# Attention, a mixture of experts and a maxout block on one core: where weight sums, conversions, Sinkhorn and pieces of expert 0 are placed

## The chip, the cores and the metric

One core of one Trainium2 chip. The metric is the device time of one execution in microseconds; the kernel of before was timed three times. Changes of less than about 0.2% are not told from no change.

## The reference

```python
attn = softmax(scale * q @ k.T + bias, local window and global keys) @ v     # 2 x 8 heads x 768 x 64
x = attn.transpose(0, 2, 1, 3).reshape(1536, 512)
logits = x @ w_gate; P = exp(logits - logits.max())                          # 1536 x 8
for _ in range(8):                                                           # Sinkhorn
    P /= P.sum(1, keepdims=True) + 1e-9
    P /= P.sum(0, keepdims=True) + 1e-9
    P *= N / E
out = sum(P[:, e:e+1] * (relu(x @ w1[e]) @ w2[e]) for e in range(8))         # 512 -> 1024 -> 512
h = max(out @ m1, out @ m2, out @ m3); y = h @ w_out                         # 512 -> 768 -> 512
```

The last block's weights come as 64-bit floats in memory and are turned into 32-bit floats on the chip.

## The kernel before

Every matmul factor is split into a high part (a copy, rounded to fp32r, on ScalarE) and a low part (the rest, by a subtraction: `lower`), and a product of two factors is three matmuls.

**The front** (`near_attention`, 49 steps s) runs the attention. From step 9 on, each of its steps takes one piece of **expert 0** from the list `todo`: `e0_pieces(tb, ...)` gives for one block `tb` of 256 tokens four pieces of the first matrix (24 matmuls of 256 columns) and then pieces of the second (`mm2`; in the front 4 pieces of 12 matmuls of 512 columns). Blocks 0 to 3 run wholly in the front. Of block 4 only the first matrix does, so the last four steps (45 to 48) have no piece. Block 5, and the second matrix of block 4, come after the front; their hidden values lie in columns of `xh`/`xl` that belonged to tokens done with.

**The main part** is an order written out by hand, in slots s. Experts 1 to 7 (two passes over halves of the tokens, p = 0 and 1, 28 groups each) and the last block (p = 2 and 3, 9 groups each) form groups G = 0 to 73. A group multiplies a 2 x 2 block matrix in the Strassen-Winograd way: seven products (`product`, line 1130) of 6 matmuls of 384 columns, at slots 7G + 0, 2, 4, 8, 10, 12, 13 (`REL`). Products 1, 2 and 4 take raw blocks of the weights (`sb`), products 3, 5, 6 and 7 take sums of them (`sa`, needed first at slot 7G + 4). With two groups in flight nearly every slot holds one product. After a slot's product come its hooks (`at(slot, f, pri)`, lower pri first) and then at most one **filler**, in order, from the slot it is due: first the 16 pieces (6 matmuls of 512 columns) of expert 0 that were left over, from slot 24 on the second matrices of experts 1 to 7 (`y_piece`, 12 per 14 slots, the last at slot 411), then 6 transposes (`x2_tile`), and late ones of the output (`o_piece`). From slot 412 to 462 hardly a filler is due.

For group G: `s_add` (slot 7G - 7) makes the four sums on POOL from the raw buffer into a tile of their own, `s_raw` (slot 7G - 5) splits the raw blocks, `s_sum` (slot 7G - 1) splits the sums; `lower` is on VectorE, for the raw blocks of p >= 2 on POOL. All loads go through one list of jobs, sorted by slot, on the SP queue: `feed` issues the next job while fewer than 4 of the 4 buffers `raw` are taken and the job's slot of readiness has come; `done` gives a buffer back and feeds.

`convert` (24 times, lines 1078 to 1104: eight VectorE instructions and a store, spread over 6 slots) turns a half of a 64-bit weight block into 32 bits, one every 7 slots from slot 15. `chain_at(p, ...)` makes four differences t1 to t4 of blocks of the tokens for pass p on POOL (line 366) in four raw buffers within 7 slots and stores them; `put` splits them for use at the pass's start (`base` = slots 0, 196, 392, 455).

**Sinkhorn**: `sink_max` (a maximum on VectorE, `partition_all_reduce` on POOL, line 902) stands after the third piece of block 5, `sink_start` at slot 4, and turn n has a small matmul `col` (line 917, into a bank of the pair b2) one slot before `turn` (lines 920 to 893 on VectorE), at slots 6 to 24, two or three apart. The first `y_piece` ends at slot 26 with an instruction that reads the result `pm`. `scale` (POOL, line 1307) multiplies expert 0's output by its column of `pm`, for the first six tiles all at slot 25.

## Time and profile before

| | |
|---|---|
| median of 3 runs | 1410.22 us (1408.98 to 1411.53) |
| the profiled execution | 1409.96 us, span 1408.0 us |
| TensorE (PE) busy | 1329.5 us, 94% of the span |
| VectorE (DVE), ScalarE (ACT), POOL busy | 921.2, 703.9, 673.3 us |
| mean granted TensorE clock | 0.971 of full speed |
| moved by DMA | 147.66 MB, 105 GB/s in the mean |

The span runs from the first to the last instruction; about 2 us of the execution lie outside it. PE is the engine that is nearly always busy, so what counts is where it is not, and which engine it waits for there. A clock of 1.00 in a row is 2.4 GHz, 0.50 is 1.2 GHz.

### The profile page before, as it was taken

To read this page: it belongs to the slowest core of one execution; us is meant where nothing else is said; L and a number is where in the kernel's file an instruction comes from. 1 tells how busy PE (TensorE), PEld (TensorE's weight loads), DVE (VectorE), ACT (ScalarE), POOL (GpSimd) and SP (SyncE) were. 2 spreads that over 40 slices of the span, in tenths; PEclk is the share of its full clock that TensorE was granted. 3 is DMA by queue.
4 is the path that set the end of the run, shared out by engine and by line. 5 is a ranking of instruction groups with operands and counts; after the bars stand their busy time and mean duration, and the time that the engine had idled before them with its cause. 6 is when DMAs were issued, how large, how long until landed. Compare 5 with 4: busy or idle time off the path is not lost.

```text
span 1408.0 us, 19757 instructions
## 1 busy us (share of the span) xinstructions
PE 1329.5 (94%) x6984; PEld 1199.3 (85%) x6984; DVE 921.2 (65%) x1513; ACT 703.9 (50%) x1415; POOL 673.3 (48%) x746
## 2 busy tenths in 40 slices
PE   5899997979999969999999999999999999988988
PEld 3789996768898868888898988889898888887977
DVE  7977875578899969898855444545454546465361
ACT  6877774444445424444465445444444455434341
POOL 5554663226445554445444433346334444595461
PEclk8899997999999989999999999999999999999999
DMA  4633532313333353334333222225211224344111
GB/s 154 180 110 96 165 124 65 120 57 113 105 123 120 111 171 113 114 120 128 121 108 105 60 90 76 76 67 159 88 61 60 64 89 138 98 146 147 60 46 45
DMA packets 59627, 147.66 MB, mean 105 GB/s; under 512 B 6016, under 2 KB 23680, under 8 KB 59520
## 3 DMA queue, kind: packets, MB, share of 16 engines
q1 hardware_dynamic: 59520, 146.32, 33.2%
q8 instruction: 57, 0.93, 0.3%
q14 instruction: 50, 0.41, 0.1%
HBM read 124.27 MB, written 22.02 MB: 104 GB/s over the span
## 4 chain that ended last, share of the span: by engine, by line
PE 82%; DVE 7%; POOL 5%; ACT 2%; DMA 2%; issue 2%; SPq 0%; POOLq 0%; DVEq 0%; ACTq 0%
PE yp L238 40%; PE b L1130 31%; PE hp L221 5%; PE o L592 2%; POOL sum L989 2%; PE t L566 2%; PE s L506 1%; POOL sbl L961 1%; DMA raw<-w 1%; POOL xl L154 1%; DVE w2l L961 1%; DVE sal L961 1%; PE lp L297 0%; DVE sbl L961 0%; DVE etl L574 0%
## 5 line engine op out<-in xcount | busy, mean ns | idle before, releaser
L154 POOL TENSOR_TENSOR xl<-u,xh 128x384 fp32r<-128x384 f32 x112 | 124.0, 1108 | 395.7 <-ACT xh L153 394.6
L238 PE MATMUL yp<-w2h,xl 128*128 128x512 f32 x744 | 296.1, 398 | 0.0
L238 PE MATMUL yp<-w2l,xh 128*128 128x512 f32 x744 | 294.8, 396 | 0.0
L238 PE MATMUL yp<-w2h,xh 128*128 128x512 f32 x744 | 290.9, 391 | 0.0
L1138 ACT COPY u<-b 128x384 f32<-128x384 f32 x148 | 70.9, 479 | 204.5 <-PE b L1130 201.8
L238 PEld LDWEIGHTS yp<-w2h,xl 128*128 128x128 f32 x744 | 140.1, 188 | 29.9
L989 POOL TENSOR_TENSOR sum<-raw 128x256 f32<-128x256 f32 x148 | 121.9, 845 | 76.9 <-DVE sal L961 48.1
L238 PEld LDWEIGHTS yp<-w2h,xh 128*128 128x128 f32 x744 | 140.7, 189 | 18.4
L238 PEld LDWEIGHTS yp<-w2l,xh 128*128 128x128 f32 x744 | 140.2, 188 | 18.4
L1228 DVE SCALAR_TENSOR_TENSOR y<-yp,pm,y 128x512 f32<-128x512 f32 x168 | 124.6, 742 | 28.9 <-PE yp L238 28.8
L961 DVE TENSOR_TENSOR w2l<-raw,w2h 128x1024 fp32r<-128x1024 f32 x62 | 90.6, 1461 | 64.4 <-ACT w2h L1013 64.4
L226 DVE SCALAR_TENSOR_TENSOR xl<-b,xh 128x384 fp32r<-128x384 f32 x56 | 31.1, 555 | 121.6 <-ACT xh L225 120.9
L154 POOL TENSOR_TENSOR xl<-s,xh 128x384 fp32r<-128x384 f32 x56 | 64.4, 1150 | 78.7 <-ACT xh L153 69.0
L961 DVE TENSOR_TENSOR sal<-sum,sah 128x1024 fp32r<-128x1024 f32 x74 | 95.3, 1288 | 8.9 <-ACT sah L995 8.9
L1158 ACT ACTIVATE s<-s 128x384 f32<-128x384 f32 x56 | 29.5, 526 | 140.7 <-DVE s L1178 140.7
L1138 ACT COPY s<-b 128x384 f32<-128x384 f32 x74 | 35.5, 479 | 125.4 <-PE b L1130 125.2
L1178 DVE TENSOR_TENSOR u<-b,u 128x384 f32<-128x384 f32 x136 | 74.8, 550 | 30.6 <-PE b L1130 30.6
L1178 DVE TENSOR_TENSOR s<-b,s 128x384 f32<-128x384 f32 x68 | 37.4, 551 | 76.4 <-PE b L1130 76.2
L995 ACT CAST sah<-sum 128x1024 fp32r<-128x1024 f32 x74 | 77.3, 1045 | 4.9 <-POOL sum L989 4.9
L989 POOL TENSOR_TENSOR sum<-raw,sum 128x256 f32<-128x256 f32 x74 | 73.9, 999 | 5.8
L1013 ACT CAST w2h<-raw 128x1024 fp32r<-128x1024 f32 x62 | 64.9, 1047 | 9.5 <-DMA raw<-w 9.4
L461 POOL TENSOR_TENSOR k<-kqv,k 128x384 fp32r<-128x384 f32 (+1 forms) x46 | 47.1, 1025 | 46.7 <-ACT k L460 46.7
(276 smaller groups left out, 3689.4 us busy)
## 6 DMA issues: line engine op xcount, KB each, us to landing
raw<-w SPq DMA_DIRECT2D x154, 512.0 KB, 3.6
kqv<-a SPq DMA_DIRECT2D x32, 416.0 KB, 3.3
raw<-xt SPq DMA_DIRECT2D x16, 384.0 KB, 3.3
w<-cb SPq DMA_DIRECT2D x24, 256.0 KB, 2.4
raw<-x2d SPq DMA_DIRECT2D x14, 384.0 KB, 3.3
xt<-raw SPq DMA_DIRECT2D x12, 384.0 KB, 2.6
kqv<-a SPq DMA_DIRECT2D x14, 320.0 KB, 3.1
w0r<-w SPq DMA_DIRECT2D x8, 512.0 KB, 3.9
```

The lines of the kernel that those rows point to most:

```text
L154: lo_eng.tensor_tensor(out=lo, in0=src, in1=hi.bitcast(F32), op=ALU.subtract)
L221: nc.tensor.matmul(ps, a[:, q], b, start=k == 0, stop=k == 11)
L238: nc.tensor.matmul(ps, a, b, start=kf == first and i == 0, stop=kf == last and i == 2)
L461: nc.gpsimd.tensor_tensor(out=kb[:, 0:nk], in0=rk, in1=ka[:, 0:nk].bitcast(F32), op=ALU.subtract)
L961: (eng or nc.vector).tensor_tensor(out=l, in0=src, in1=h.bitcast(F32), op=ALU.subtract)
L989: nc.gpsimd.tensor_tensor(out=o, in0=a, in1=b, op=op)
L995: nc.scalar.copy(h, r)
L1013: nc.scalar.copy(h, r)
L1130: nc.tensor.matmul(s[BANK[m]], a[:, c], b[:, kk], start=k == 0 and m in FIRST, stop=k == 5 and m in LAST, skip_group_check=True,)
L1138: nc.scalar.copy(t, st[G]["b1"])
L1178: nc.vector.tensor_tensor(out=o, in0=s[b], in1=s[nm], op=ALU.add)
L1228: nc.vector.scalar_tensor_tensor(out=y[n], in0=ps, scalar=pm[:, n, e : e + 1], in1=y[n], op0=ALU.mult, op1=ALU.add)
```

## The change

- **Sums in place.** `sum_up` makes the four sums in the raw buffer itself, in an order that needs no other tile, so the blocks of sums stand in another order (`PROD`). `s_raw` now comes first (slot 7G - 7), `s_add` at 7G - 5, `s_sum` at 7G - 2, and the raw buffer is held until then. The tile of sums goes and a fifth raw buffer takes its place.
- **Sums of the last block ahead.** For its nine weight blocks the sums are made once, during the passes (`sums_m`, slots 50, 78, ..., 274: a load, four POOL instructions, a store to `w32s`), and each of the 18 last groups loads them as a second job instead of adding. The low part of the sums goes to POOL for every third of these groups.
- **Conversions** come every 14 slots instead of 7 (slots 15 to 337).
- **Chains** of passes 1 and 2 take one difference every 28 slots, that of pass 3 one every 4; each difference loads its two blocks anew (eight loads instead of four).
- **Sinkhorn**: `sink_max` stands first after the front, `sink_start` ahead of slot 0, the `col`s at slots 1, 4, 7, 10, 13, 17, 20, 24 in bank b3, each `turn` first among the hooks of the next slot. `scale` of the first six tiles is spread over slots 25 to 35.
- **Expert 0**: block 4's second matrix runs in the front (4 pieces, steps 45 to 48); block 5's 8 pieces are due at slots 0, 2, ..., 14.

```diff
@@ -244,9 +244,10 @@
     def e0_pieces(tb, php, pyp):
         box = {}
         ws = [w0[4 + j][0] for j in range(4)]
-        if tb >= 4:
-            f = slice((tb - 4) * 2048, (tb - 3) * 2048)
-            box["h"], box["l"] = [t[:, f].rearrange("p (f n) -> p f n", f=8) for t in (xh, xl)]
+        if tb == 5:
+            box["h"], box["l"] = [
+                t[:, 0:2048].rearrange("p (f n) -> p f n", f=8) for t in (xh, xl)
+            ]
 
         def mm1(i):
             def go():
@@ -633,7 +634,7 @@
                         if tb < 5:
                             l1, l2 = logits(tb, ps_h)
                             p1, (p2, _) = e0_pieces(tb, lambda: ps_h, lambda: ps_y)
-                            pcs = p1 + p2 if tb < 4 else p1
+                            pcs = p1 + p2
                             todo += [l1, pcs[0], l2] + pcs[1:]
                             light = (l1, l2)
                 split_qk(s + 2)
@@ -821,13 +822,13 @@
             for tb in range(6):
                 for go in logits(tb, ps_h):
                     go()()
-            for tb in range(5):
-                p1, (p2, _) = e0_pieces(tb, lambda: ps_h, lambda: ps_y)
-                for go in p1 + p2 if tb < 4 else p1:
-                    go()()
             for f in chain0():
                 if f:
                     f()
+            for tb in range(5):
+                p1, (p2, _) = e0_pieces(tb, lambda: ps_h, lambda: ps_y)
+                for go in p1 + p2:
+                    go()()
 
 
     with tc.If(far == 0) as cmp:
@@ -842,9 +843,8 @@
 
 
     tpool = ctx.enter_context(tc.tile_pool(name="tpool", bufs=1))
-    rpool = ctx.enter_context(tc.tile_pool(name="rpool", bufs=4))
+    rpool = ctx.enter_context(tc.tile_pool(name="rpool", bufs=5))
     mpool = ctx.enter_context(tc.tile_pool(name="mpool", bufs=1))
-    upool = ctx.enter_context(tc.tile_pool(name="upool", bufs=1))
     cpool = ctx.enter_context(tc.tile_pool(name="cpool", bufs=3))
     late = ctx.enter_context(tc.tile_pool(name="late", bufs=1))
     ps_b1 = ctx.enter_context(tc.tile_pool(name="ps_b1", bufs=3, space=PSUM))
@@ -913,7 +913,7 @@
         box = {}
 
         def col():
-            box["ps"] = bank("b2", "c")
+            box["ps"] = bank("b3", "c")
             nc.tensor.matmul(box["ps"][:, 0:E], ones, cs[:, 0], start=True, stop=True)
 
         def turn():
@@ -936,7 +936,7 @@
         job_l.append((slot, len(job_l), key, src, shape, ready))
 
     def feed():
-        while job_q and flying["n"] < 4 and job_q[0][3] <= flying["slot"]:
+        while job_q and flying["n"] < 5 and job_q[0][3] <= flying["slot"]:
             key, src, k2, _ = job_q.pop(0)
             r = rpool.tile([128, 1024], F32, tag="raw", name="raw")
             if k2 == "x":
@@ -962,11 +962,16 @@
 
 
     ops_ = [{} for _ in groups]
-    sums = {}
-
-    def s_done(G):
-        if len(ops_[G]) == 2:
-            done(("s", G))
+    w32s = dpool.tile([9, 128, 1024], F32, name="w32s")
+
+    def sum_up(r):
+
+        b = [r[:, 256 * i : 256 * i + 256] for i in range(4)]
+        for o, x, z, op in (
+            (2, 3, 2, ALU.add), (3, 0, 3, ALU.subtract), (0, 2, 0, ALU.subtract),
+            (1, 1, 0, ALU.subtract),
+        ):
+            nc.gpsimd.tensor_tensor(out=b[o], in0=b[x], in1=b[z], op=op)
 
     def s_raw(G):
         h, l = new_slot(spool, "sb", 768, "sb")
@@ -974,34 +979,42 @@
         nc.scalar.copy(h, r)
         lower(h, l, r, nc.gpsimd if groups[G][0] >= 2 else nc.vector)
         ops_[G]["b"] = (h, l)
-        s_done(G)
 
     def s_add(G):
-        ops_[G]["a"] = new_slot(spool, "sa", 1024, "sa")
-        sums[G] = upool.tile([128, 1024], F32, tag="sum", name="sum")
-        r4 = jobs["s", G].rearrange("p (b n) -> p b n", b=4)
-        s4 = sums[G].rearrange("p (b n) -> p b n", b=4)
-        for o, a, b, op in (
-            (s4[:, 0], r4[:, 3], r4[:, 2], ALU.add), (s4[:, 2], r4[:, 0], r4[:, 3], ALU.subtract),
-            (s4[:, 1], s4[:, 0], r4[:, 0], ALU.subtract),
-            (s4[:, 3], r4[:, 1], s4[:, 1], ALU.subtract),
-        ):
-            nc.gpsimd.tensor_tensor(out=o, in0=a, in1=b, op=op)
-        s_done(G)
+        sum_up(jobs["s", G])
 
     def s_sum(G):
-        h, l = ops_[G]["a"]
-        r = sums.pop(G)
-        nc.scalar.copy(h, r)
-        lower(h, l, r)
+        h, l = new_slot(spool, "sa", 1024, "sa")
+        p, e, i = groups[G]
+        key = ("s" if p < 2 else "ss", G)
+        nc.scalar.copy(h, jobs[key])
+        lower(h, l, jobs[key], nc.gpsimd if p >= 2 and i % 3 == 2 else nc.vector)
+        ops_[G]["a"] = (h, l)
+        done(key)
 
     for G, (p, e, i) in enumerate(groups):
         s = 7 * G - 7
         job(s, ("s", G), w1[e, i] if p < 2 else w32[i])
+        if p >= 2:
+            job(s + 3, ("ss", G), w32s[i])
         if G > 1:
-            at(s, lambda G=G: s_add(G))
-            at(s + 2, lambda G=G: s_raw(G))
-            at(s + 6, lambda G=G: s_sum(G))
+            at(s, lambda G=G: s_raw(G))
+            if p < 2:
+                at(s + 2, lambda G=G: s_add(G))
+            else:
+                at(s, lambda G=G: done(("s", G)), 3)
+            at(s + 5, lambda G=G: s_sum(G))
+
+    def sums_m(u):
+        r = jobs["su", u]
+        sum_up(r)
+        nc.sync.dma_start(out=w32s[u], in_=r)
+        done(("su", u))
+
+    for u in range(9):
+        s = 28 * u + 50
+        job(s, ("su", u), w32[u], None, s - 8)
+        at(s, lambda u=u: sums_m(u))
 
 
     ws = {}
@@ -1035,17 +1048,30 @@
         for nm, r in USE.items():
             t = nm in XT
             src = xt[p][XT.index(nm)] if t else x_block(xd if p < 2 else x2d, p, nm)
-            job(base[p] - 6 + r, ("x", p, nm), src, "t" if t else "x", (-9, 102, base[1] + 109, base[2] + 43)[p])
+            job(base[p] - 6 + r, ("x", p, nm), src, "t" if t else "x", (-9, 177, base[1] + 185, base[2] + 48)[p])
             if base[p] - 6 + r >= 0:
                 at(base[p] - 6 + r, lambda p=p, nm=nm: put(p, nm))
 
 
-    def chain_at(p, s, src):
-        for o, nm in zip((0, 0, 2, 6), ("b11", "b12", "b22", "b21")):
-            job(s + o, ("c", p, nm), x_block(src, p, nm), "x", s - 8)
-        c = chain(p, lambda nm: jobs["c", p, nm][:, 0 : 2 * QT], lambda nm: done(("c", p, nm)))
-        for i, f in enumerate(c):
-            at(s + 2 * i, f)
+    SUM = (("t1", "b12", "b11"), ("t3", "b22", "b12"), ("t2", "b22", "t1"), ("t4", "b21", "t2"))
+
+    def chain_at(p, s, d, src):
+        for n, (o, a, b) in enumerate(SUM):
+            for x in (a, b):
+                t = x in XT
+                job(
+                    s + n * d, ("c", p, n, x), xt[p][XT.index(x)] if t else x_block(src, p, x),
+                    "t" if t else "x", s + n * d - (d - 1 if t and d < 8 else 8),
+                )
+
+            def go(n=n, o=o, a=a, b=b):
+                ra, rb = [jobs["c", p, n, x][:, 0 : 2 * QT] for x in (a, b)]
+                nc.gpsimd.tensor_tensor(out=ra, in0=ra, in1=rb, op=ALU.subtract)
+                nc.sync.dma_start(out=xt[p][XT.index(o)], in_=ra)
+                for x in (a, b):
+                    done(("c", p, n, x))
+
+            at(s + n * d, go)
 
 
     def x2_tile(t, tag):
@@ -1109,8 +1135,8 @@
 
 
     PROD = {
-        1: ("b", 0, "b11"), 2: ("b", 1, "b21"), 3: ("a", 3, "b22"), 4: ("b", 2, "t4"),
-        5: ("a", 0, "t1"), 6: ("a", 1, "t2"), 7: ("a", 2, "t3"),
+        1: ("b", 0, "b11"), 2: ("b", 1, "b21"), 3: ("a", 1, "b22"), 4: ("b", 2, "t4"),
+        5: ("a", 2, "t1"), 6: ("a", 0, "t2"), 7: ("a", 3, "t3"),
     }
     BANK = {1: "b1", 6: "b1", 7: "b1", 4: "b1", 5: "b2", 3: "b2", 2: "b3"}
     FIRST, LAST = (1, 5, 2), (4, 3, 2)
@@ -1290,18 +1316,17 @@
 
 
     for n in range(24):
-        convert(n // 2, n % 2, 7 * (n + 2) + 1)
-    chain_at(1, 94, xd)
+        convert(n // 2, n % 2, 14 * n + 15)
+    chain_at(1, 92, 28, xd)
     for t in range(6):
         at(base[1] + 43 + 7 * t, lambda t=t: x2_tile(t, "b2"))
-    chain_at(2, base[1] + 101, x2d)
-    chain_at(3, base[2] + 35, x2d)
-
-    at(4, sink_start)
-    for n in range(1, SINK + 1):
-        col, turn = sink_turn(n)
-        at(4 + 5 * n // 2 - 1, col)
-        at(4 + 5 * n // 2, turn)
+    chain_at(2, 288, 28, x2d)
+    chain_at(3, base[2] + 36, 4, x2d)
+
+    for n, c in enumerate((1, 4, 7, 10, 13, 17, 20, 24)):
+        col, turn = sink_turn(n + 1)
+        at(c, col)
+        at(c + 1, turn, -1)
 
     def scale(t):
         nc.gpsimd.tensor_scalar(
@@ -1309,17 +1334,17 @@
         )
 
     for t in range(NTT):
-        at(25 if t < 6 else 30 + 7 * t, lambda t=t: scale(t), 1)
+        at(25 + 2 * t if t < 6 else 30 + 7 * t, lambda t=t: scale(t), 0)
 
 
     job_q += [j[2:] for j in sorted(job_l, key=lambda j: j[:2])]
     feed()
     p1 = e0_pieces(5, lambda: Banks("b1"), None)[0]
     early = {
-        3: (lambda: s_raw(0), lambda: put(0, "b11")),
+        3: (sink_max, lambda: s_raw(0), lambda: put(0, "b11")),
         0: (lambda: s_add(0), lambda: put(0, "b21")),
-        1: (lambda: s_sum(0), lambda: put(0, "t2"), sink_max),
-        2: (lambda: s_raw(1),),
+        1: (lambda: s_raw(1), lambda: put(0, "t2")),
+        2: (lambda: s_sum(0), sink_start, lambda: s_add(1)),
     }
     ev = None
     for i in (3, 0, 1, 2):
@@ -1329,13 +1354,10 @@
         for f in early[i]:
             f()
     ev()
-    at(0, lambda: s_add(1))
-    at(6, lambda: s_sum(1))
-
-    mm2 = []
-    for tb in (5, 4):
-        mm2 += e0_pieces(tb, None, lambda: Banks("yp"))[1][1]
-    fillers[:0] = [(0, lambda s, f=f: at(s + 1, f(), 1)) for f in mm2]
+    at(5, lambda: s_sum(1))
+
+    mm2 = e0_pieces(5, None, lambda: Banks("yp"))[1][1]
+    fillers[:0] = [(2 * i, lambda s, f=f: at(s + 1, f(), 1)) for i, f in enumerate(mm2)]
 
 
     s = 0
```

## Rows read from the trace of the kernel before

**Rows 1.** The page, part 2: busy tenths of PE in 40 slices.
```profile
PE   5899997979999969999999999999999999988988
```

**Rows 2.** Waits of PE: engine, line <- whom; us in total, times, longest.
```profile
PE c L917 <- DVE cs L893: 14.4, 5, 5.2
PE b L1130 <- POOL sbl L961: 14.4, 7, 3.4
PE b L1130 <- DVE u L1178: 13.4, 4, 11.5
```

**Rows 3.** Stretches: length, busy us and count of PE, PEld, DVE, ACT, POOL; clock, DMA share, GB/s.
```profile
254.40:319.00 64.60, 50.15 (x235) 43.95 (x233) 38.25 (x93) 25.49 (x44) 19.10 (x23) 0.92 0.26 83
...
491.00:518.00 27.00, 15.48 (x73) 13.81 (x72) 13.86 (x18) 7.16 (x13) 14.05 (x11) 0.81 0.51 144
518.00:1210.70 692.70, 692.70 (x3460) 622.68 (x3460) 428.44 (x557) 336.01 (x581) 311.36 (x313) 1.00 0.31 98
1210.70:1278.00 67.30, 58.72 (x319) 55.99 (x317) 43.01 (x52) 33.31 (x57) 51.14 (x46) 0.95 0.44 137
1278.00:1408.00 130.00, 116.93 (x576) 105.58 (x575) 50.74 (x67) 44.28 (x75) 56.17 (x52) 0.97 0.20 68
219.60:238.20 18.60, 12.59 (x58) 10.27 (x56) 9.61 (x26) 8.60 (x23) 3.93 (x7) 0.62 0.07 22
268.00:272.00 4.00, 3.88 (x11) 3.12 (x12) 3.76 (x11) 0.33 (x1) 0.00 (x0) 0.58 0.71 256
```

**Rows 4.** The chain that ended last: start, us, what (x matmuls).
```profile
901.24 1.39 PE yp L238 x6
926.99 3.12 PE b L1130 x18
```

**Rows 5.** Two stretches, matmuls of the products (line 1130) alone: PE, PEld, clock, DMA.
```profile
254.40:319.00 64.60, 25.75 (x120) 23.32 (x120) 0.92 0.26 83
1210.70:1408.00 197.30, 126.19 (x654) 118.09 (x654) 0.97 0.28 92
```

**Rows 6.** The same stretches, matmuls of the second matrices (line 238) alone.
```profile
254.40:319.00 64.60, 26.27 (x96) 18.72 (x96) 0.92 0.26 83
1210.70:1408.00 197.30, 52.80 (x216) 41.31 (x216) 0.97 0.28 92
```

**Rows 7.** Timeline of DVE: first and last instruction of one turn (eight in all).
```profile
292.99 0.16 DVE L920 TENSOR_SCALAR cs<-c 128x8 f32<-128x8 f32 x1
...
294.76 0.34 DVE L893 TENSOR_REDUCE cs<-pm 128x8 f32<-128x96 f32 x1
```

**Rows 8.** Timeline of POOL before slot 4: start, us, what, [idle before <- releaser].
```profile
254.36 0.38 POOL L902 PARTITION_ALL_REDUCE mx<-mx  x1 [7.16 <-DVE sbl L961]
262.44 0.72 POOL L989 TENSOR_TENSOR sum<-raw 128x256 f32<-128x256 f32 x1 [7.71 <-issue]
```

**Rows 9.** Last stage, sums (line 989) alone: POOL busy (count), clock, DMA share, GB/s.
```profile
1210.70:1278.00 67.30, 22.50 (x28) 0.95 0.44 137
1278.00:1408.00 130.00, 23.71 (x29) 0.97 0.20 68
```

**Rows 10.** Groups of POOL by shape: count | busy us, mean ns | idle before.
```profile
L961 POOL TENSOR_TENSOR sbl<-raw,sbh 128x768 fp32r<-128x768 f32 x18 | 34.8, 1935 | 5.7 <-ACT sbh L974 5.7
...
L366 POOL TENSOR_TENSOR raw<-raw 128x768 f32<-128x768 f32 x12 | 23.9, 1994 | 11.3 <-DMA raw<-xd 6.0 <-DVE ct L1079 5.2
```

**Rows 11.** Groups of DVE by shape: the low part of the sums.
```profile
L961 DVE TENSOR_TENSOR sal<-sum,sah 128x1024 fp32r<-128x1024 f32 x74 | 95.3, 1288 | 8.9 <-ACT sah L995 8.9
```

**Rows 12.** Timelines of POOL and ACT near 500 us.
```profile
494.25 1.93 POOL L366 TENSOR_TENSOR raw<-raw 128x768 f32<-128x768 f32 x1 [5.99 <-DMA raw<-xd]
...
504.68 1.05 ACT L1013 CAST w2h<-raw 128x1024 fp32r<-128x1024 f32 x1 [9.45 <-DMA raw<-w]
```

**Rows 13.** DMA issues: tiles, queue, count, KB each, median us from issue to landing.
```profile
raw<-w SPq DMA_DIRECT2D x154, 512.0 KB, 3.6
...
xt<-raw SPq DMA_DIRECT2D x12, 384.0 KB, 2.6
```

## The prediction

> **What bounds it now.** I read the slices of the page first: PE is at 90% or more nearly throughout, with holes at the start, near 230 to 320 us, near 510 us and from 1230 us on [rows 1]. The waits of PE name the holes: `col` waiting for Sinkhorn on DVE, products waiting for the low part of the raw weight blocks on POOL, and products waiting for DVE, one of these waits 11.5 us long [rows 2]. The stretches then show what each hole is worth [rows 3]. From 518 to 1210.7 us PE has no idle time at all and the clock is 1.00, so no part of the change can gain anything there; it can only lose.
>
> Work that PE must do comes from two durations at 2.4 GHz: 18 product matmuls take 3.12 us, 0.173 each, and 6 of a second matrix 1.39 us, 0.232 each [rows 4].
>
> The *opening* (slots 0 to 24, 254.4 to 319.0 us) lasts 64.6 us. It holds 120 product matmuls, 120 x 0.173 = 20.8 us [rows 5], and 96 of expert 0, 96 x 0.232 = 22.3 us [rows 6], 43.1 us in all. PE is busy 50.15 us because the clock, 0.92 in the mean, is at 1.2 GHz part of the time, and idle for 14.45 us [rows 3], which is nearly all the waiting for Sinkhorn, 14.4 us [rows 2].
>
> The *hole of the chain* (491 to 518 us): 27 us, PE busy 15.48 [rows 3], so 11.5 us idle. POOL's difference waits 6.0 us for its load and ACT 9.45 us for a load of w2 [rows 12]: the chain holds the four raw buffers, and what other loads bring is late. About 1.5 us more goes at the low clock after the wait (0.81 in the mean).
>
> The *last stage* (1210.7 us to the end) lasts 197.3 us. 654 product matmuls are 113.4 us [rows 5], 216 of the output 50.1 us [rows 6]; with some 2.6 us of transposes (an estimate: 24 of them beside matmuls that cost 0.1 to 0.2) and about 3.6 us of drain that makes 169.7 us, so 27.6 us are lost, 13.6 of them before 1278 us. There POOL is busy 51.1 of 67.3 us [rows 3], 22.5 of it with sums [rows 9].
>
> **The change part by part**, against the profiled span of 1408.0 us (execution 1409.96, within 0.3 us of the median 1410.22).
>
> *Block 4's second matrix goes to the front.* 48 matmuls x 0.232 = 11.1 us leave the opening. They land in steps 45 to 48 (219.6 to 238.2 us), where PE is busy 12.59 of 18.6 us at clock 0.62 [rows 3], so its work there is about 12.59 x 0.62 = 7.8 us at the full clock. 7.8 + 11.1 = 18.9 us fits 18.6 if the clock stays up. The last chain to the logits remains behind it. I take +2 us; bounds -1 (the clock also stays up for block 5's first matrix) and +6 (half of the pieces uncovered). The two copies to `y` ride on ACT, which is half idle in this stretch [rows 3].
>
> *The opening.* PE's work falls from 43.1 to 32.0 us. DVE is busy 38.25 us there [rows 3]: a turn takes 295.10 - 292.99 = 2.1 us [rows 7], up to 2.8 where a row of it is slow, and there are seven whole ones. The second conversion and `sink_start` leave the stretch, so about 35 us remain: **DVE becomes the longer engine**. Each turn is now first in its slot and the next `col` two or three slots on, where it was behind puts, splits and adds. Lower bound 35 us (DVE alone). Upper bound: the two engines' work over the time stays as it was, (43.1 + 38.25)/64.6 = 1.26, so (32.0 + 35)/1.26 = 53 us, and 4 us for a new wait below: 57. Two prices lie between. The `col`s now share the single bank b3 with product 2, so four pairs wait for DVE's add of 0.55 us and its signal: some 3 us. And the all-reduce on POOL is moved ahead of `s_add(0)`: after it POOL stands still for 7.71 us for nothing that the profile shows [rows 8], so 8.1 us come before the sums that slot 4 needs, then four sums at 0.8 [rows 9], then split and `sink_start`; `col` 1 in slot 1 waits 1 to 4 us. The GPSIMD Engine Reference of the Trainium skill (2.1, Instruction dispatch) gives a first call of a freshly loaded POOL kernel about 6 us of loading that no instruction shows; the row is somewhat longer, and by the page `col` 1 would wait 1.7 us less. I take 49.6 us, nearer to the upper bound because PE and DVE still take turns: **-15 us** (bounds -30 and -7.6).
>
> *Chains of passes 1 and 2 spread, five buffers.* Each difference holds two buffers instead of up to four, 28 slots (62 us) apart; four loads more per chain. The hole of 11.5 + 1.5 = 13 us goes. For new waits, 1 us: **-12 us** (bounds -13 and 0).
>
> *Conversions over both passes*: 24 x about 7 us of DVE spread from the first pass over both. In the long stretch DVE is busy 428 of 693 us [rows 3]; what moves is at most 12 x 7 = 84 us. Nothing on PE's path: 0. If that cover were gone, adds would come late for PE's banks.
>
> *Sums in place*: the raw buffer is held from slot 7G - 7 to 7G - 2, three slots longer; the fifth buffer pays for it, and conversions take half as many in the first pass. `s_sum` follows `s_add` by three slots (6.7 us) for 3.2 us of POOL work, with two slots more to spare at its end than it needs. 0.
>
> *Sums ahead*: nine loads, 36 POOL instructions x 0.8 = 29 us and nine stores in the passes, where POOL is busy 311 of 693 us [rows 3]. SP is in order, so each store waits there for POOL, and loads queue behind it: 3.2 us of sums, 2.6 for a store, 3.6 for the load into the freed buffer [rows 13], about 10 us. Four other buffers are loaded ahead, at some six loads per 14 slots (31 us) worth 20 us (14 slots hold 84 product matmuls and 72 of a second matrix: 84 x 0.173 + 72 x 0.232 = 31.2 us, 2.23 a slot). So hidden: 0, counted with the rivals.
>
> In the last stage POOL loses 57 sums, 46.2 us [rows 9], and gains six low parts of 1024 columns. None stands in the trace; by the 768-column row, 1.935 x 4/3 = 2.6 us on POOL [rows 10], against 1.288 on DVE [rows 11]; 15.6 us in all. Before 1278 us POOL falls from 51.1 to 51.1 - 22.5 + 2 x 2.6 = 34 us of 54 us of PE work. **What is late next is a load.** That part moved 137 GB/s x 67.3 us = 9.2 MB [rows 3]; seven loads of sums (0.52 MB each) and four more loads of chain 3 (0.39) make 14.5 MB. In 60 us that is 240 GB/s, against 256 at a share of 0.71 in the busiest row [rows 3]. Chain 3 makes it worse: differences 4 slots (4.2 us) apart of 2.0 us on POOL [rows 10], each store waited for by SP, and t1 and t2 loaded back right after they were stored. I leave 6 of the 13.6 us lost before 1278 us and 6 of the 14 after: **-15 us** (bounds -27 and 0).
>
> *`scale` spread, bank orders*: 0.
>
> **Sum**: 2 - 15 - 12 - 15 = -40 us; 1410 - 40 = 1370 us.
>
> **The rivals.**
> *Loads bind the last stage.* For it: the 240 GB/s above, and SP in order. Against: shares of 0.44 and 0.20 leave room [rows 3]. At 200 GB/s the 14.5 MB take 72.5 us instead of 61: 1370 + 12 = 1382.
> *The opening stays a ping-pong.* For it: neither engine was full before, 50 and 38 of 64.6 us [rows 3]. Against: the longest waits were for `cs`, whose place improves. 57 instead of 49.6 us: 1378.
> *Slower: SP's new stores starve the passes.* 17 stores in the passes (nine of sums, eight of chains) that SP must wait for. For it: in the hole, four chain steps cost 13 us, 3.3 each. Against: there all four buffers were taken. It decides when fewer than 10 us of loads lie ready, that is at two buffers ahead. 17 x 3.3 = 56 us: 1426. From 2.4 us each on, the change is slower.
> *The last stage does not want what the sums gave it*: DVE or ACT take POOL's place there and the opening gains only its bound of 7.6: about 1392.
>
> **How the numbers follow.** Forecast 0.56, loads 0.18, ping-pong 0.14, starved passes 0.06, the last one 0.06. The forecast's own range is 1355 to 1380; the two middle rivals reach 1390 together. So 1354 to 1392 leaves out little but the slower rival and the ends of the bounds. A change of 0.2% (2.8 us) is about what can be told from none: faster 0.91, same 0.02, slower 0.07.
>
> **What would show it.** The waits of PE: `col` <- DVE well under 14.4 us, products <- POOL `sbl` gone, no wait of 11 us. Stretches: slot 0 near 256 us, slot 24 near 306, the last stage near 182 us, with a DMA share above 0.7 in its first 60 us; PE idle nowhere between. It is wrong if PE idles in the passes at slots 28u + 57 (stores of sums) or if the last stage stays near 197 us.

## The result and the profile after

The changed kernel takes **1376.34 us** (1374.88 to 1377.7, 4 runs) against 1410.49: a ratio of 0.9759, interval 0.9742 to 0.9775, so 34 us faster. The forecast was 1370, with a range of 1354 to 1392. The profiled execution took 1376.38 us, span 1374.6.

The page of after, parts 1 and 2 (busy time of the engines; PE in 40 slices, to be held against [rows 1]):

```profile
PE 1319.0 (96%) x6984; PEld 1190.9 (87%) x6984; DVE 948.5 (69%) x1507; ACT 700.8 (51%) x1415; POOL 645.9 (47%) x716
...
PE   5899999879999999999999999999999999979998
```

Of the three holes, the one near 510 us is gone, the one of the opening is shorter, and one in the last stage is left. The waits of PE in after, where before had [rows 2]:

```profile
PE b L1156 <- ACT u L1164: 8.1, 5, 4.9
PE b L1156 <- DVE cs L920: 8.1, 3, 6.9
PE t L567 <- POOL nn L553: 4.5, 6, 1.3
PE b L1156 <- DVE u L1204: 4.1, 3, 1.7
PE hp L221 <- issue: 3.3, 1, 3.3
PE c L917 <- DVE cs L893: 3.1, 2, 2.8
```

`col` waits 3.1 us instead of 14.4, no product waits for the raw blocks' low part on POOL any more, and the wait of 11.5 us is gone. Two waits are new, and each takes the place of an old one: product 2 waits for a *turn* of Sinkhorn to read its bank (8.1 us), and product 4 waits for ScalarE (1.75, 0.83 and 4.89 of the 8.1 us).

Stretches of after, in the columns of [rows 3], cut at the same slots (a slot is found in the timeline by the first matmul of its product):

```profile
256.10:308.40 52.30, 38.90 (x184) 34.45 (x184) 40.42 (x94) 24.86 (x43) 18.47 (x20) 0.87 0.34 108
...
219.60:240.00 20.40, 19.75 (x121) 17.30 (x119) 11.36 (x30) 10.73 (x29) 5.21 (x9) 1.00 0.06 21
491.00:518.00 27.00, 27.00 (x137) 24.36 (x137) 19.60 (x26) 14.85 (x26) 14.95 (x17) 1.00 0.37 122
1186.70:1254.60 67.90, 57.39 (x317) 54.16 (x316) 39.41 (x50) 32.14 (x57) 35.93 (x21) 0.95 0.66 218
1254.60:1374.60 120.00, 113.50 (x578) 102.98 (x576) 45.97 (x64) 43.64 (x75) 35.65 (x25) 1.00 0.29 102
```

| stretch | before, us | after, us | difference | forecast |
|---|---|---|---|---|
| up to slot 0 | 254.5 | 256.2 | +1.7 | +2 |
| opening, slot 0 to 24 | 64.6 | 52.3 | -12.3 | -15 |
| passes, slot 24 to 413 | 891.7 | 878.2 | -13.5 | -12 |
| last stage, slot 413 to 462 | 67.0 | 67.9 | +0.9 | -7.6 |
| last stage, slot 462 to the end | 130.2 | 120.0 | -10.2 | -8 |
| sum | 1408.0 | 1374.6 | -33.4 | -40 |

Two stretches need an explanation: why the opening still lasts 52.3 us when PE has 32 us of work there, and why the first part of the last stage gained nothing although POOL's load in it fell from 51.1 to 35.9 us.

**The opening.** After's DVE (first rows) and PE (last row) at slot 17 to 23:

```profile
297.59 1.23 DVE L961 TENSOR_TENSOR w2l<-raw,w2h 128x1024 fp32r<-128x1024 f32 x1 [0.95 <-ACT w2h L1026]
298.74 0.42 DVE L1112 TENSOR_SCALAR ct<-ct 128x512 int32<-128x512 int32 x1
...
302.33 1.21 DVE L961 TENSOR_TENSOR w2l<-raw,w2h 128x1024 fp32r<-128x1024 f32 x1
...
304.17 1.37 DVE L1126 TENSOR_TENSOR cb<-cb,cs 128x512 f32<-128x512 f32 x1
305.57 0.69 DVE L1127 SCALAR_TENSOR_TENSOR cb<-cb,ct 128x512 f32<-128x512 f32 x1
306.18 0.16 DVE L920 TENSOR_SCALAR cs<-c 128x8 f32<-128x8 f32 x1
...
306.39 0.69 PE L1156 MATMUL b<-b21h,sbh 128*128 128x384 f32 x1 [6.94 <-DVE cs L920]
```

DVE works without a pause from 297.6 to 306.2 us, through two splits of w2, a split of sums and the rest of the first conversion, before it comes to the turn. Until that turn has read bank b3, product 2 can't write there. And at the opening's start, POOL of after:

```profile
243.52 0.38 POOL L902 PARTITION_ALL_REDUCE mx<-mx  x1 [14.08 <-DVE mx L899]
252.82 7.75 POOL L974 TENSOR_TENSOR raw<-raw 128x256 f32<-128x256 f32 x8 [8.93 <-DVE xl L226]
```

8.9 us pass between the all-reduce and the first sums, as 7.7 did in [rows 8], now ahead of group 0's sums. The first 1.9 of them are another wait: these sums are made in place, so they can start only when DVE's split of group 0's raw blocks has ended, at 245.80 us. 7.0 us remain.

**The last stage.** After's SP queue, ACT and PE near slot 446:

```profile
1228.20 0.32 SPq L945 DMA_DIRECT2D raw<-xt  x1
1228.57 0.42 SPq L949 DMA_DIRECT2D raw<-w  x1
...
1232.52 0.83 ACT L979 CAST sbh<-raw 128x768 fp32r<-128x768 f32 x1 [2.82 <-DMA raw<-w]
...
1233.79 0.69 PE L1156 MATMUL b<-t4h,sbh 128*128 128x384 f32 x1 [4.89 <-ACT u L1164]
```

A load of weights is issued late, behind one of chain 3: SP had waited 3.7 us for POOL's third difference, to store it, and then 2.0 us for the store to land, to load it back. ACT waits 2.82 us for the weights with the split `s_raw`, and the evacuation `u` that frees product 4's bank stands behind that split in ACT's order.

### The profile page after: what moved, and what is told of

It is laid out like the page before. It is cut to its first block, busy times and chain, and to the rows that moved or that the text cites. A ratio compares the mean times of both kernels' runs of the same rounds, so it can differ in the third digit from the quotient of the medians.

```text
span 1374.6 us, 19793 instructions
## 1 busy us (share of the span) xinstructions
PE 1319.0 (96%) x6984; PEld 1190.9 (87%) x6984; DVE 948.5 (69%) x1507; ACT 700.8 (51%) x1415; POOL 645.9 (47%) x716
## 4 chain that ended last, share of the span: by engine, by line
PE 88%; DVE 5%; ACT 2%; issue 2%; DMA 1%; POOL 1%; DVEq 0%; SPq 0%; POOLq 0%; ACTq 0%
PE yp L238 42%; PE b L1156 35%; PE hp L221 5%; PE o L593 2%; PE t L567 2%; PE s L507 1%; DVE sal L961 1%; POOL raw L1069 0%; PE lp L298 0%; DMA x2d<-x2t 0%; DMA raw<-xt 0%; ACT sbh L979 0%; PE x L1081 0%; DVE u L1204 0%; DMA raw<-w 0%
## 5 line engine op out<-in xcount | busy, mean ns | idle before, releaser
L154 POOL TENSOR_TENSOR xl<-u,xh 128x384 fp32r<-128x384 f32 x112 | 115.8, 1034 | 349.7 <-ACT xh L153 345.3
L974 POOL TENSOR_TENSOR raw<-raw 128x256 f32<-128x256 f32 x260 | 230.7, 888 | 74.1 <-DVE sbl L961 49.0
L1254 DVE SCALAR_TENSOR_TENSOR y<-yp,pm,y 128x512 f32<-128x512 f32 x168 | 124.3, 740 | 15.5 <-PE yp L238 15.4
L961 DVE TENSOR_TENSOR sbl<-raw,sbh 128x768 fp32r<-128x768 f32 x56 | 75.2, 1342 | 62.9 <-ACT sbh L979 61.4
L961 DVE TENSOR_TENSOR sal<-raw,sah 128x1024 fp32r<-128x1024 f32 x68 | 84.6, 1244 | 25.6 <-ACT sah L990 25.5
L961 DVE TENSOR_TENSOR w2l<-raw,w2h 128x1024 fp32r<-128x1024 f32 x62 | 83.0, 1338 | 13.2 <-ACT w2h L1026 13.2
L154 POOL TENSOR_TENSOR xl<-s,xh 128x384 fp32r<-128x384 f32 x56 | 59.7, 1066 | 53.6 <-ACT xh L153 53.6
L990 ACT CAST sah<-raw 128x1024 fp32r<-128x1024 f32 x74 | 77.3, 1044 | 4.5 <-POOL raw L974 2.5
L1184 ACT ACTIVATE u<-u 128x384 f32<-128x384 f32 x112 | 59.1, 528 | 24.0 <-DVE u L1204 24.0
L979 ACT CAST sbh<-raw 128x768 fp32r<-128x768 f32 x74 | 61.5, 832 | 10.5 <-DMA raw<-w 6.0
```

The source lines that it names most:

```text
L154: lo_eng.tensor_tensor(out=lo, in0=src, in1=hi.bitcast(F32), op=ALU.subtract)
L961: (eng or nc.vector).tensor_tensor(out=l, in0=src, in1=h.bitcast(F32), op=ALU.subtract)
L974: nc.gpsimd.tensor_tensor(out=b[o], in0=b[x], in1=b[z], op=op)
L979: nc.scalar.copy(h, r)
L990: nc.scalar.copy(h, jobs[key])
L1184: nc.scalar.activation(src, src, AF.Relu)
```

## The experiments

All are told against the changed kernel (1376.3 us, opening 52.3, slot 413 to 462 67.9) or the kernel before (1410 to 1412 in the same sessions). Kernels that are alike up to there reach slot 0 at 254.2 to 256.4 us and take 12.9 to 15.9 us from slot 0 to 7, where PE's clock falls at another moment; slot 413 to 462 took 67.0 to 68.5 us where nothing in it was changed. So a difference of 1 us there, and of 3 us before slot 7, says nothing by itself.

**e1: chain 3 as before, each block loaded once.**
```diff
-    chain_at(3, base[2] + 36, 4, x2d)
+    chain_once(3, base[2] + 35, x2d)     # the chain_at of before
```


> The changed kernel, but the chain of pass 3 as before: four blocks loaded once and kept in their buffers, differences two slots apart. Theory (each difference's store holds SP until POOL is done, the loads of stored differences wait for their stores, and so the loads of the last groups' weights come late): the stretch from slot 413 to 462 falls from 67.9 us to about 60, ACT's waits for raw<-w there (3.2 and 2.8 us) go, and the time falls from 1376 to about 1369 us. Rival (the raw blocks' split now stands two slots earlier in ACT's order, and whatever it waits for holds up the evacuations behind it): the same within 2 us.

1375.8 us, ratio 0.9747 (0.9725 to 0.9769): no change. Slot 413 to 462 takes 68.0 us. The wait has only moved, to slot 439; ACT and PE of e1:

```profile
1224.05 0.83 ACT L979 CAST sbh<-raw 128x768 fp32r<-128x768 f32 x1 [8.79 <-DMA raw<-w]
...
1225.31 0.69 PE L1164 MATMUL b<-t4h,sbh 128*128 128x384 f32 x1 [6.41 <-ACT u L1172]
```

My theory fell in this form: the loads done twice are not the cause. With four blocks held instead, the weights' load comes later still. The rival's chain of waits is the same in both. The stretch moved 196 GB/s here and 218 in after, in the same time, so the bytes are not what it waits for.

**e5: no chain 3 at all** (the four differences of pass 3 are left out, and its products read those of pass 2).
```diff
-    chain_at(3, base[2] + 36, 4, x2d)
...
-            src = xt[p][XT.index(nm)] if t else ...
+            src = xt[min(p, 2)][XT.index(nm)] if t else ...
```


> The changed kernel without the four differences of pass 3 (no loads, no POOL work, no stores for them; its products read those of pass 2). Theory (chain 3 takes the buffers, SP and POOL when the last groups' weights must be loaded): slot 413 to 462 falls from 67.9 us to 55 to 57, near its work of 53.7, and the time from 1376 to about 1365 us. Rival (the added loads of sums, or ACT's order, bind that stretch by themselves): it stays above 63 us.

1367.85 us, ratio 0.9687 (0.9667 to 0.9707). The stretch of slot 413 to 462 in e5:

```profile
1187.40:1245.90 58.50, 54.67 (x317) 52.94 (x316) 35.52 (x50) 32.00 (x57) 26.32 (x17) 1.00 0.57 173
```

58.5 us instead of 67.9. So chain 3 costs 9.4 us there, in whichever form, and without it the loads of the sums ahead can be carried: PE idles 58.5 - 54.7 = 3.8 us.

**e6: the raw blocks' split in the last stage two slots later**, as before.
```diff
-            at(s, lambda G=G: s_raw(G))
+            at(s if p < 2 else s + 2, lambda G=G: s_raw(G))
...
-                at(s, lambda G=G: done(("s", G)), 3)
+                at(s + 2, lambda G=G: done(("s", G)), 3)
```


> The changed kernel, but in the last stage the split of the raw blocks stands at slot 7G - 5 again, as before the change, instead of 7G - 7. Theory (ACT waits in order for a load of weights and the evacuations behind it come late): each such wait has two slots (2.1 us) more, PE's waits for ACT in the stretch from slot 413 to 462 (1.8, 0.8 and 4.9 us) shrink to about 3 us in all, the time falls by 3 to 5 us. Rival (the loads are late by themselves, whoever waits first): PE waits for the low part on POOL instead, the same time within 2 us.

1370.91 us, ratio 0.9712 (0.9694 to 0.9729). The stretch of slot 413 to 462 in e6:

```profile
1182.10:1246.40 64.30, 58.70 (x317) 56.03 (x316) 36.23 (x50) 32.58 (x57) 35.38 (x21) 0.95 0.72 233
```

64.3 us, 3.6 less, with the same bytes at 233 GB/s; PE's waits for ACT's `u` shrink from 7.6 us in four to one of 1.2 us, and 1.9 us for POOL's `sbl` come back. Slot 462 to 511 takes 78.6 us instead of 80.1, which six other kernels with the early split show as well, to 0.1 us. Together that is 5.2 us, and the median fell by 5.4: the theory's size and a little more. (This profile is 9.3 us shorter than after's, because slot 0 also comes 1.6 us earlier and slot 0 to 4 takes 8.9 us instead of 10.9, at a clock of 1.00 instead of 0.72, with nothing changed there.)

**e8: no sums ahead.** The last stage's sums are made in place from each group's raw buffer, four POOL instructions for each of 18 groups, with all low parts on DVE.
```diff
-        if p >= 2:
-            job(s + 3, ("ss", G), w32s[i])
...
+            at(s + 2, lambda G=G: s_add(G))
...
-    for u in range(9): ...                   # sums_m
```


> The changed kernel, but the sums of the last stage are made there again (in place, four POOL instructions for each of the 18 groups), none ahead, and their low parts are all on DVE. Theory (the sums ahead took POOL off the path from slot 462 on, but filled DMA and buffers up to there): slot 462 to 511 rises from 80.1 to about 88 us, slot 413 to 462 stays at 65 to 70, the time rises to about 1383 us. Rival (the stretch up to 462 is bound by the loads of sums): that stretch falls to about 60 us and the time stays near 1376.

1388.4 us, ratio 0.9829 (0.981 to 0.9848), 12 us slower than with them. Stretches of e8, slot 413 to 462 and slot 462 to 511:

```profile
1186.20:1260.50 74.30, 61.81 (x317) 58.27 (x316) 45.19 (x53) 33.00 (x57) 57.43 (x48) 0.91 0.48 156
1260.50:1345.40 84.90, 78.41 (x403) 71.17 (x403) 43.94 (x53) 34.48 (x59) 45.48 (x43) 1.00 0.23 76
```

POOL is busy 57.4 of 74.3 us. So the sums ahead are worth 74.3 - 67.9 = 6.4 us in the first part and 84.9 - 80.1 = 4.8 in the second. This run gives POOL its work back together with taking the loads away, so it does not price the loads alone; it shows that the sums ahead save more than their loads cost. This run also says where the gain of the first part went: e8 needs 74.3 us there and the kernel before 67.0, so the rest of the change costs 7.3 us in this stretch, and the sums ahead give 6.4 back. What in the rest it is (the split two slots earlier in ACT's order, the sums in place, which wait for the split, chain 3's new form) was not taken apart in e8; in the changed kernel e6 gives 3.6 us to the first and e1 nothing to the last. In slot 462 to 511 the rest of the change gains instead, 88.4 us before against 84.9.

**e2: Sinkhorn's matmul in the pair of banks b2.**
```diff
-            box["ps"] = bank("b3", "c")
+            box["ps"] = bank("b2", "c")
```


> The changed kernel, but Sinkhorn's small matmul writes to a bank of the pair b2 again instead of the single bank b3. Theory (DVE is the longer engine of the opening, its queue is full until 308 us): PE's wait of 6.9 us at product 2 in slot 23 comes back at the next col or the first pieces of y, slot 0 to 24 stays at 50 to 53 us, and the time within 2 us of 1376. Rival (sharing bank b3 is itself the cost, 8.1 us of waits): slot 0 to 24 falls to 44 to 46 us and the time to about 1369.

1374.57 us, ratio 0.975 (0.9726 to 0.9775): no change that can be told. Product 2's wait is gone, but in e2's waits of PE `col` has

```profile
PE c L917 <- DVE cs L893: 10.8, 5, 4.6
```

in place of 3.1: the last `col` of slot 24 waits for the same turn. Slot 24's product itself came early (44.2 us after slot 0), slot 28's 61.4 us after it against 64.0. The single bank is where the wait shows, not what makes most of it; at most some 2.6 us are its own.

**e3: conversions 14 slots later, the sums ahead 21.**
```diff
-        convert(n // 2, n % 2, 14 * n + 15)
+        convert(n // 2, n % 2, 14 * n + 29)
-        s = 28 * u + 50
+        s = 28 * u + 71
```


> The changed kernel, but every conversion 14 slots later (from slot 29) and the sums ahead 21 slots later, so that no conversion runs in the opening. Theory (DVE is the longer engine there): about 6 us of DVE work leave it, slot 0 to 24 falls from 52.3 to 46 to 48 us, the time to about 1371 us. Rival (bank b3, or the latency of the turns): 52 us as before, 1376.

1368.39 us, ratio 0.9699 (0.9677 to 0.9721), 8 us less. The opening of e3, then its wait of PE for the turns:

```profile
254.10:298.90 44.80, 36.99 (x185) 32.54 (x184) 34.04 (x80) 24.88 (x43) 18.03 (x20) 0.96 0.31 98
```
```profile
PE b L1156 <- DVE cs L920: 3.4, 3, 2.3
```

44.8 us instead of 52.3: 6.4 us less DVE (34.0 instead of 40.4) gave 7.5 us at slot 24; 2 of them are lost again by slot 28, in part to a lower clock there (0.75 against 0.84), so 5.6 us last (58.4 instead of 64.0 from slot 0 to 28). DVE's queue is on the opening's path. It is not full (40.4 of 52.3 us), so PE waits for turns that stand behind other work in that queue, not for an engine without a pause.

**e4: one more all-reduce at the start**, its result unused.
```diff
+    nc.gpsimd.partition_all_reduce(warm[:, 1:2], warm[:, 0:1], 128, RED.max)
     ident = const.tile([128, 128], F32, name="ident")
```


> The changed kernel with one more all-reduce over two numbers on POOL at the kernel's start; its result is not used. Theory (the 8.9 us for which POOL stands still after the all-reduce are paid once, with the first call): at the second call POOL goes on within 2 us, the sums of group 0 come some 6 us earlier, slot 0 to 7 falls from 15.2 to about 11 us, the time by 3 to 5 us. The front may lose up to 8 us if POOL is needed there at once; then the time stays. Rival (the all-reduce itself takes this long): POOL stands still for 8 to 9 us again and the time is the same or worse.

1384.8 us, ratio 0.9813 (0.9786 to 0.984), 8 us slower: slot 0 comes 8.9 us later, and slot 0 to 7 takes 14.4 us, not 11. POOL of e4, around the first all-reduce and after the second, then the split on DVE that the sums at 262.05 us overwrite the input of:

```profile
9.10 0.38 POOL L103 PARTITION_ALL_REDUCE warm<-warm  x1 [5.57 <-issue]
9.35 0.27 POOL masks.py:197 MEMSET ident<- 128x128 f32 x1
...
10.36 0.21 POOL L110 CAST wg<-wgr 128x32 fp32r<-128x32 f32 x1
17.77 0.24 POOL L111 TENSOR_TENSOR wg<-wgr,wg 128x32 fp32r<-128x32 f32 x1 [7.19 <-issue]
...
252.02 0.38 POOL L906 PARTITION_ALL_REDUCE mx<-mx  x1 [13.98 <-DVE mx L903]
262.05 7.63 POOL L978 TENSOR_TENSOR raw<-raw 128x256 f32<-128x256 f32 x8 [9.65 <-DVE sbl L965]
...
254.30 0.96 DVE L965 TENSOR_TENSOR sbl<-raw,sbh 128x768 fp32r<-128x768 f32 x1 [2.42 <-DMA raw<-xd]
```

The gap is not paid once. At the start 5.6 us pass before the all-reduce and 7.2 before the first two-input instruction after it, with fills and a copy running freely between; at the second all-reduce 9.65 us pass again, 6.8 of them after that split has ended (255.26 us). So the theory was wrong, and the rival in part: it is not the all-reduce that lasts, but the first TENSOR_TENSOR behind it that comes late, both times.

**e7: no all-reduce.** Each partition subtracts its own rows' maximum; Sinkhorn's first row sums divide it out.
```diff
-        nc.gpsimd.partition_all_reduce(mx[:, 1:2], mx[:, 0:1], 128, RED.max)
...
-        nc.vector.tensor_scalar_mul(mx[:, 1:2], mx[:, 1:2], -1.0)
+        nc.vector.tensor_scalar_mul(mx[:, 1:2], mx[:, 0:1], -1.0)
```


> The changed kernel, but each partition subtracts the maximum of its own rows instead of the maximum over all (the first row sums of Sinkhorn divide it out again), so that there is no all-reduce on POOL. Theory (after the all-reduce POOL stands still for about 9 us, and the sums of group 0 and the first col wait for it): POOL sums start near 246 us instead of 252.8, slot 0 to 7 falls from 15.2 to 10 to 12 us, and the time by 3 to 5 us. Rival (DVE is the bound of the opening whatever comes first): slot 24 comes no more than 1 us earlier.

1371.17 us, ratio 0.9712 (0.9696 to 0.9728), 5 us less. POOL of e7:

```profile
247.46 4.37 POOL L973 TENSOR_TENSOR raw<-raw 128x256 f32<-128x256 f32 x4 [17.11 <-DMA raw<-xd]
253.96 4.71 POOL L973 TENSOR_TENSOR raw<-raw 128x256 f32<-128x256 f32 x4 [2.12 <-DVE sbl L960]
```

Group 0's sums start 5.4 us earlier, 0.1 us after DVE's split of group 0 has ended, and slot 0 to 7 takes 9.8 us instead of 15.2. All of it stays: from slot 7 to 24 both kernels take 37.1 us. Slot 0 to 7 of after, then of e7:

```profile
256.20:271.40 15.20, 12.13 (x48) 10.38 (x47) 8.56 (x22) 6.80 (x11) 5.14 (x6) 0.78 0.26 78
```
```profile
257.10:266.90 9.80, 9.52 (x48) 8.11 (x47) 7.10 (x22) 5.86 (x10) 2.50 (x3) 1.00 0.31 100
```

In after the first `col` waits 2.8 us there, in e7 not at all; the other 2.6 us are PE's, at a mean clock of 0.78 instead of 1.00. The clock does not always fall with that wait: e6 has it too (3.0 us) and takes 12.9 us. So the all-reduce costs the opening some 3 us by its wait, and up to 6 with the clock.

**e9: the kernel before with the spread chains alone.**
```diff
-    chain_at(1, 94, xd)
+    chain_far(1, 92, 28, xd)             # the chain_at of after
...
-    chain_at(2, base[1] + 101, x2d)
+    chain_far(2, 288, 28, x2d)
```


> The kernel before with one part of the change: the differences of passes 1 and 2 taken 28 slots apart, each from blocks loaded anew; four buffers, conversions every 7 slots and all else as before. Theory (the hole near 500 us is the chain's own, four blocks in four buffers): slot 98 to 112 falls from 45.5 us to about 31.3, the time from 1410 to about 1396 us. Rival (the fifth buffer or the halved conversions are needed as well): a good part of the hole stays, 1403 us or more.

1401.9 us, ratio 0.9944 (0.9929 to 0.9959). Slot 98 to 112 in e9:

```profile
490.90:523.60 32.70, 31.85 (x157) 28.00 (x156) 31.50 (x41) 16.50 (x28) 19.22 (x16) 1.00 0.42 132
```

32.7 us instead of 45.5 (31.3 in after). Spreading the chain closes the hole; the fifth buffer and the halved conversions are needed only for the last 1.5 us there and 1.6 us that e9 loses between slot 112 and 196, where DVE still has twice the conversions. The time fell by 9 us only, between theory and rival: those 1.6 us, and in this profile 2.2 in the last stage and 1.3 up to slot 24, where nothing was edited, go off the 12.8, and 1.4 between slot 24 and 98 come to it.

But four blocks in four buffers do not make a hole by themselves. The kernel before takes the chain of pass 2 in the same way at slots 297 to 303, and PE has no idle time around it:

```profile
935.00:985.00 50.00, 50.00 (x249) 44.73 (x249) 27.23 (x34) 23.59 (x41) 28.04 (x26) 1.00 0.40 127
```

Beside the chain of pass 1 conversions run, which take buffers and DVE too and end at slot 181; beside that of pass 2 they do not. Fewer conversions with the old chain was not run, so which share is theirs is not shown.

**e10: the kernel before with block 4's second matrix in the front alone** (and block 5's pieces at every second slot).
```diff
-                            pcs = p1 + p2 if tb < 4 else p1
+                            pcs = p1 + p2
...
+    fillers[:0] = [(2 * i, lambda s, f=f: at(s + 1, f(), 1)) for i, f in enumerate(mm2)]
```


> The kernel before with another part of the change: block 4's second matrix in the front, block 5's eight pieces at slots 0, 2 to 14. Theory (in the opening PE and DVE take turns, so PE work that leaves is time): slot 0 comes 1 to 2 us later, slot 24 about 9 us earlier, 1402 us. Rival (the opening is bound by Sinkhorn on DVE, and PE only waits more for it): slot 24 comes less than 4 us earlier, 1407 us or more.

1405.57 us, ratio 0.9966 (0.9952 to 0.9979). Slot 0 comes 1.2 us later; the opening, in e10,

```profile
255.60:314.00 58.40, 42.93 (x186) 38.21 (x186) 40.75 (x93) 24.34 (x42) 19.02 (x22) 0.82 0.29 93
```

lasts 58.4 us instead of 64.6. 11.1 us of PE work taken away gave 6.2 us: between the theory and the rival. PE waits more for `cs` (15.5 us), and works at a lower mean clock (0.82).

**e11 and e12: three and four edits together** (e3, e6 and e7; then e2 too).

> The changed kernel with three of the edits together: conversions 14 slots later, no all-reduce, the raw blocks' split of the last stage at slot 7G - 5. If their causes are apart, their gains add: slot 0 to 24 about 39 us (52.3 less 7.6 and 5.4), slot 413 to 462 about 64, the time about 1360 us. Rival (both edits of the opening relieve the same DVE queue): slot 0 to 24 43 us or more and 1364.

> The last kernel with Sinkhorn's matmul in the pair of banks b2 as well. Theory (with DVE's queue shorter, the waits for the single bank b3 at product 2, 0.9 and 2.3 us, are now costs of their own): 2 to 3 us less than the kernel with three edits. Rival (they come back at the next col): the same within 1 us.

e11 takes **1359.57 us**, ratio 0.9635 (0.9622 to 0.9648); e12 1358.41 us, 0.9631 (0.9617 to 0.9644). The opening of e11:

```profile
256.50:297.50 41.00, 36.28 (x184) 32.19 (x183) 33.51 (x83) 23.94 (x42) 14.98 (x17) 0.97 0.36 116
```

41.0 us and 64.0 for slot 413 to 462: the gains add, but for 2 us at slot 24; at slot 28 these are there as well (12.2 us less than after, where e3 has 5.6 and e7 6.0). Both beat both kernels, by 17 us the one after. e12's gain over e11 lies within the runs' spread, so nothing is claimed for the bank.

## Why the prediction was right, and where it was off

- **Front, +2 forecast, +1.7 measured.** The reason held: with the pieces in it the stretch has PE busy 19.75 of 20.40 us at clock 1.00, where it was 0.62 [rows 3].
- **Opening, -15 forecast, -12.3 measured.** That PE now waits for work in DVE's queue is shown by e3; DVE is not full, so PE and DVE still take turns, as the forecast had it. The new wait for the all-reduce, put at 1 to 4 us, was 2.8; taking the all-reduce away gave 5.4 (e7), because the clock stayed up as well, which the sum did not have. Two terms were mis-sized. "Some 3 us" for bank b3 in four waits became 8.1 in three; e2 shows that most of these are DVE's, not the bank's. And the work left on DVE, taken as 35 us, was 40.4.
- **Chains and buffers, -12 forecast, -13.5 measured over the passes** (14.2 at the hole itself). e9 shows that spreading the chain gives most of it. The reason given, four held buffers, is not the whole one: in the chain of pass 2 they cost nothing, and the sum's 12 us came from pass 1 alone. Nothing was lost to the 17 new stores: PE has no idle time from 491 to 518 us, and none of 0.3 us or more from 320 to 1186 us, the end of the passes. The rival of starved passes is out.
- **Sums ahead, the step that failed: "I leave 6 of the 13.6 us lost before 1278 us".** All of it stayed, 67.9 - 53.7 = 14.2 us. That a load would be late next was right, as was the demand: 218 GB/s at a share of 0.66, where 240 were estimated. But the number of bytes did not make it: e1 moves fewer in the same time, e6 the same in 3.6 us less, and without chain 3 the loads of sums fit into 58.5 us (e5). What the sum had at nothing, the raw blocks' split moved ahead of the sums and two slots earlier, is one part (3.6 us by e6): ACT waits in order, and a late load there holds PSUM banks, which POOL, where the wait was before, does not. Chain 3, which the prediction named but left room for, is the other (9.4 us by e5; the kernel before had it as well). No run has both taken away, so whether the two add is not shown. Its blame on the repeated loads was wrong (e1); which of its buffers, its POOL time or its hold of SP counts most was not taken apart and stays open.
- **Second part of the last stage, -8 forecast, -10.2 measured.** POOL was the bound there, as [rows 2, 9] said: products waited 8.9 us for its low part of the raw blocks from slot 462 on, and wait no more. But only 4.8 of the 10.2 us are shown to come from the sums made ahead (e8, up to slot 511). In e8, where POOL makes the sums again, that wait is gone too; the likely reason is that the split now stands ahead of the sums in POOL's order, a part that the sum had at nothing, but no run has it alone. The low parts on POOL took 2.4 us each by after's groups, estimated at 2.6:

```profile
L961 POOL TENSOR_TENSOR sal<-raw,sah 128x1024 fp32r<-128x1024 f32 x6 | 14.4, 2401 | 19.9 <-ACT sah L990 18.6 <-PE b L1156 1.3
```

So the forecast's size held in four stretches of the five; in the fifth the rival that loads bind the last stage came about halfway. Of its two reasons the bytes are not it; the other, SP in order, is seen in the trace near slot 446 and was not tested apart. The total is some 7 us off and not 11 because the passes and the second part of the last stage gained 3.7 us more than forecast, the latter in part for a reason that the prediction did not have: that is luck.

## What to carry to other kernels

Where engines wait in order, moving a step from one engine's place to another's also moves the wait it begins with: put first, in the queue that frees PSUM, only what is surely there. A wait's label names who ended it, not what made it: the bank that PE waited for was a reader late in DVE's queue, and taking work from that queue gave what another bank did not. And where few buffers serve many kinds of loads, a step that holds several of them at once is best spread: for pass 1, with conversions beside it, four differences 28 slots apart gave 12.8 us; for pass 2, with none beside it, there was nothing to gain.

## What was not expected of the hardware

Behind an all-reduce POOL stands still for some 7 us before its next two-input instruction, each time anew: 7.2 and 6.8 us in e4, 7.7 in the kernel before, 7.0 in after, where the second and the last count from the end of the DVE split that the sums also wait for (the whole idle times are 9.65 and 8.93). Fills and a one-input copy behind the first one are not held up. Before the first all-reduce of e4, which nothing else holds up, POOL stands still for 5.6 us; before the second, behind 14 us of idle time, none of it shows. The GPSIMD Engine Reference of the Trainium skill (2.1, Instruction dispatch) puts some 6 us on the first call of a freshly loaded kernel; the 5.6 us before the first all-reduce agree with it, and the gap on the way back, and its return at the second all-reduce, are what e4 adds.
